# Two neighbouring tokens per partition and 64x64 tiles in the first two batches of a retention and swish kernel

## The chip, the cores and the metric

The kernel runs on one core of a Trainium2 chip, in bf16 matmuls on f32 data from HBM. The metric is device time in microseconds (us) of one execution; smaller is better. Engines: PE (matrix), PEld (its weight loads), DVE (vector), ACT (scalar), POOL (gpsimd) and SP, which issues DMAs.

## The reference

```python
def _attn_ref(q, k, v):                      # q, k, v: 8 batches, 8 heads, 576 tokens, 64
    scores = scale * np.matmul(q, k.transpose(0, 1, 3, 2))
    gamma = 1.0 - 2.0 ** (-5.0 - np.arange(H, dtype=np.float32))
    Dmat = np.where(rel >= 0, gamma[:, None, None] ** rel[None, :, :], 0.0)
    return np.matmul(scores * Dmat, v)
def _moe_ref(x, w_in, w_out, beta):          # x: 4608 x 512; w_in 512 x 2048; w_out 2048 x 512
    h = x @ w_in
    return (h * (1.0 / (1.0 + np.exp(-beta * h)))) @ w_out
```

The first is attention without a softmax, with a decay per head (gamma to the distance, causal). Its heads are laid side by side into x, which goes through two matrices with a swish between them.

## The kernel before

Each batch's first 512 tokens are a block; the last 64 tokens of all eight batches make a ninth block, in four pairs. Attention is done in chunks of 128 tokens. The decay splits into a gain on q (gq) and one on v (gv), so a chunk needs: scores of keys against queries inside the chunk (`a_sc`, tile sc), a causal mask on DVE that also evicts sc from PSUM into R (L332), R times v (`a_O`, tile O), and what earlier chunks add through a 64x64 state per head (`a_cross`). The state is the sum of k times v of the chunks so far (`a_st`, tile st, one PSUM buffer), evicted to sbuf by ACT or DVE after each chunk (L408, L416). O goes to xT (`a_x`), the input of the MLP.

Of q a partition holds four neighbouring tokens (1024-byte runs, `load_q`, L82). Of k and v a partition holds one token of each head, 256-byte runs (`load_kv`, L94). POOL casts k to bf16 (L277) and scales v (L259), DVE scales q in batches 0 and 1 (L251). In these two batches PE turns q and k (`t_q` L301, `t_k` L307) and ACT or DVE evicts (L302, L308); for later batches DMA transposes do it. In batches 0 and 1 a_st multiplies two heads by two heads, 128x128, and keeps the two diagonal blocks; sbd holds them for a_cross with zeros beside them. Later batches use 128x64 tiles for st (L402) and O (L441) and 64x64 tiles for the cross part (L453).

The MLP of a block is `up` (64 matmuls of 512 columns into 16 tiles ph, L473, and a swish on ACT into gT, L475; `up_pair`, L488 and L491, for batch 0's first two tiles) and `down` (64 into 4 tiles po, L506, evicted by L513). Weights come in eight pieces of w_in (L177) and four of w_out (L192), cast by POOL and DVE (L185, L188) or scaled by 1/beta (L200 POOL, L202 ACT, L204 DVE). All loads and most stores go through SP's queue in the order of the code: q, k and v of batch 0, w_in, then w_out, then batch 1 and 2.

The order is written by hand. Batch 0's attention stands as a list of calls, with a few matmuls on a zero tile between them (`warm_up`, L212). After it a list `fill` holds the MLP steps of all blocks; a step is four 512-column matmuls, or four of 256 columns for batch 1's halved up. `merged` walks through fill, and ahead of step n it makes all calls of `streams` that are due (a number at most n). d0 is the index of batch 0's first down step, u1 that of batch 1's first up step (d0 + 16). Each engine takes its own instructions in this order.

```python
    fill += [F(up, 1, fo, 2 * x, 2) for x in range(2) for fo in range(10)]
    fill += [F(up, 1, fo) for fo in range(10, FO)]
```

So batch 1's up takes ten tiles in halves, the first half of the tokens and then the second, and six whole.

Of the kernel before, what the change touches and what calls it, by code (L numbers as in the profile page):

```python
# [19 lines left out]
def kernel(  # L20
# [21 lines left out]
    PC = P // CB  # L42
    TL = S - MB
# [23 lines left out]
    NQ = 6  # L67
    E = CB
# [4 lines left out]
    def load_q(b, us=(0, 1)):  # L73
# [6 lines left out]
        for u in us:  # L80
            w = slice(u * HP, (u + 1) * HP)
            nc.sync.dma_start(t[:, w].rearrange("p h i d -> p h (i d)"),  # L82
                              q[b, w, :MB, :].rearrange("h (p i) d -> p h (i d)", i=CB))

# [12 lines left out]
    ahead = [(0, 0), (0, 1), (1, 0), (1, 1), (2, 0), (3, 0), (2, 1), (3, 1)]  # L97
    keys_first = [(0, 0), (1, 0), (0, 1), (1, 1), (2, 0), (3, 0), (2, 1), (3, 1)]
# [13 lines left out]
    for n, j in ahead:  # L112
        load_kv(n, (j,))
# [7 lines left out]
    pos = consts.tile([P, 2, CB + 1], F32, name="pos")  # L121
    for j, (step, mul) in enumerate(((1, CB), (P, 1))):
        nc.gpsimd.iota(pos[:, j, :CB], pattern=[[step, CB]], base=0, channel_multiplier=mul,
                       allow_small_or_imprecise_dtypes=True)
        for x in range(2):
            nc.gpsimd.iota(pos[x * TL:(x + 1) * TL, j, CB:], pattern=[[0, 1]], base=MB, channel_multiplier=1,
                           allow_small_or_imprecise_dtypes=True)
    lscale = consts.tile([P, 1], F32, name="lscale")
    nc.vector.memset(lscale[:], math.log(scale))
    lg = consts.tile([P, 2, CB + 1, H], F32, name="lg")  # L130
    for h in range(H):
        nc.vector.tensor_scalar(lg[:, :, :, h], pos[:], math.log(1.0 - 2.0 ** (-5.0 - h)), None, ALU.mult)
    gq = consts.tile([P, CB + 1, H], F32, name="gq")
    gv = consts.tile([P, CB + 1, H], F32, name="gv")
    nc.scalar.activation(gq[:], lg[:, 0], ACT.Exp, bias=lscale[:])
    nc.scalar.activation(gv[:], lg[:, 1], ACT.Exp, scale=-1.0)
# [6 lines left out]

    causal = consts.tile([P, P], BF16, name="causal")
    nc.gpsimd.memset(causal[:], 1.0)
    nc.gpsimd.affine_select(out=causal[:], in_=causal[:], pattern=[[1, CB], [CB, PC]], compare_op=ALU.is_ge,
                            fill=0.0, base=0, channel_multiplier=-1)
# [3 lines left out]
    sbds = [consts.tile([P, HP, P], BF16, name=f"sbd{i}") for i in range(NS)]  # L151
# [28 lines left out]
    def cast_w_in(g):  # L180
        t = wts[g]
        f0, fn = pieces[g]
        for ko in range(KO):
# [6 lines left out]
    def load_w_out(g):  # L190
        t = stage.tile([P, KO, d_model], F32, name="wt", tag="wt", bufs=4)
        nc.sync.dma_start(t[:], w_out_r[:, g * KO:(g + 1) * KO, :])  # L192
# [141 lines left out]
    def split(i):  # L334
        return i in (CB - 1, CB + 1)
# [392 lines left out]
```

## Time and profile before

| | |
|---|---|
| runs, median of 3 | 306.67 us (305.7 to 306.93) |
| the profiled execution | 305.54 us |
| its span, first to last instruction | 303.8 us |
| PE, PEld busy | 293.4 us (97%), 151.3 us (50%) |
| DVE, ACT, POOL busy | 108.0, 134.1, 99.9 us |
| granted PE clock | 1.0 in every slice |
| HBM read, written | 36.71 MB, 9.44 MB |

Busy matmuls overlap, so PE's share does not tell how full it is; where PE is the limit is read from the chain that ended last (followed back from the last instruction, at each step to what released it). A group's row gives code line, engine, operation, tiles, count, busy time and the mean of one in ns. A timeline row gives start, length, engine, line, operation, shapes and count; in brackets the idle time ahead of it and what ended it. A windows row gives the stretch, PE, PEld, DVE, ACT and POOL busy (with counts), granted clock, DMA share, GB/s.

### The profile page before, as it was taken

The page shows a single profiled execution, that of the slowest core. Times are in us where ns is not written, and L with a number is a line of the kernel's source. Part 1 is how long each engine was busy: PE and PEld are TensorE (multiplying, and loading weights), DVE is VectorE, ACT ScalarE, POOL GpSimd, SP SyncE. Part 2 cuts the span into 40 slices and gives each one's busy share as a digit, 9 for nine tenths or more (in the row PEclk, how much of TensorE's full clock was granted, in tenths as well). Part 3 has the DMA queues.
Part 4 walks back from the last instruction along what each step waited for, and adds up shares of the span by engine and source line. Part 5 has one row for each costly group of instructions (what it writes and reads, how often), then busy time and mean ns, then how long its engine had stood idle before and what let it go on. Part 6 is the DMA issues. An engine that isn't in the chain of part 4 may idle for free.

```text
span 303.8 us, 5689 instructions
## 1 busy us (share of the span) xinstructions
PE 293.4 (97%) x2311; PEld 151.3 (50%) x2345; DVE 108.0 (36%) x202; ACT 134.1 (44%) x227; POOL 99.9 (33%) x138
## 2 busy tenths in 40 slices
PE   7799999999999999999999999999999999999995
PEld 5544456854544454445444544454455544444444
DVE  6588566504640433133222413151346510020012
ACT  5567546781147313741374127511771058107700
POOL 4666317552840723350308030942342000000000
PEclk9999999999999999999999999999999999999999
DMA  8999999999999999908982889997996110131011
GB/s 210 219 344 363 385 252 244 237 189 243 173 249 265 233 190 230 262 12 158 252 219 66 156 226 243 214 187 184 185 200 112 60 45 0 32 73 35 2 69 69
DMA packets 129210, 53.86 MB, mean 177 GB/s; under 512 B 109968, under 2 KB 122656, under 8 KB 129184
## 3 DMA queue, kind: packets, MB, share of 16 engines
q1 hardware_dynamic: 129152, 53.49, 78.4%
q8 instruction: 18, 0.29, 0.4%
q14 instruction: 8, 0.07, 0.1%
q10 hardware_dynamic: 32, 0.01, 0.0%
HBM read 36.71 MB, written 9.44 MB: 152 GB/s over the span
## 4 chain that ended last, share of the span: by engine, by line
PE 87%; DMA 6%; SPq 4%; issue 1%; POOL 1%; DVE 0%; POOLq 0%
PE po L506 41%; PE ph L473 36%; SPq L94 3%; DMA wt<-in_moe_w_out_dram 3%; PE sc L327 3%; DMA wt<-in_moe_w_in_dram 2%; PE O L441 2%; PE st L402 2%; PE O L453 1%; SPq L177 1%; POOL w_out_sb L200 1%; PE O L376 0%; PE st L405 0%; SPq L82 0%; PE T L307 0%
## 5 line engine op out<-in xcount | busy, mean ns | idle before, releaser
L475 ACT ACTIVATE gT<-ph,beta_sb 128x512 bf16<-128x512 f32 (+1 forms) x152 | 99.5, 659 | 82.2 <-PE ph L473 81.7
L506 PE MATMUL po<-w_out_sb,gT 128*128 128x512 bf16 (+2 forms) x591 | 127.1, 368 | 2.1 <-issue 1.3
L473 PE MATMUL ph<-xT,w_in_sb 128*128 128x512 bf16 (+1 forms) x592 | 125.1, 365 | 0.8 <-issue 0.2
L473 PEld LDWEIGHTS <-w_in_sb 128*128 128x128 bf16 x608 | 58.4, 98 | 63.0 <-DVE w_in_sb L188 0.9
L506 PEld LDWEIGHTS <-gT 128*128 128x128 bf16 x608 | 56.8, 98 | 63.9 <-issue 0.6
L332 DVE TENSOR_TENSOR R<-sc,causal 128x512 bf16<-128x512 f32 x72 | 45.0, 684 | 81.4 <-PE sc L327 80.3
L513 DVE COPY ot<-po 128x512 f32<-128x512 f32 (+2 forms) x34 | 22.4, 657 | 77.2 <-PE po L506 74.4
L277 POOL CAST kn<-kvn 128x512 bf16<-128x512 f32 x32 | 19.5, 612 | 55.5 <-DMA kvn<-in_k_dram 55.1
L259 POOL TENSOR_TENSOR vn<-kvn,gv 128x512 bf16<-128x512 f32 x32 | 33.3, 1042 | 13.1 <-DMA kvn<-in_v_dram 6.3
L251 POOL TENSOR_TENSOR qs<-qn,gq 128x512 bf16<-128x512 f32 x24 | 24.3, 1042 | 35.1 <-DMA qn<-in_q_dram 35.1
L408 ACT CAST sbq<-st 128x256 bf16<-128x256 f32 x18 | 6.6, 369 | 35.8 <-PE st L402 35.8
L461 DVE CAST xT<-O 128x512 bf16<-128x512 f32 x20 | 12.7, 685 | 20.2 <-PE O L453 20.2
L327 PE MATMUL sc<-qT,kT 64*128 64x128 bf16 x256 | 10.8, 218 | 0.7 <-ACT kT L308 0.6
L188 DVE CAST w_in_sb<-wt 64x256 bf16<-64x256 f32 x32 | 10.7, 334 | 1.4 <-DMA wt<-in_moe_w_in_dram 0.3
L461 ACT CAST xT<-O 128x512 bf16<-128x512 f32 x8 | 4.7, 587 | 13.4 <-PE O L453 13.4
L327 PEld LDWEIGHTS <-kT 64*128 64x128 bf16 x288 | 8.2, 94 | 3.8 <-issue 1.7
L185 POOL CAST w_in_sb<-wt 128x256 bf16<-128x256 f32 x16 | 7.2, 469 | 5.3 <-DMA wt<-in_moe_w_in_dram 5.3
L402 PEld LDWEIGHTS <-kn 128*64 128x64 bf16 x192 | 5.1, 110 | 7.6 <-issue 6.4
L212 PE MATMUL ph<-warm 128*128 128x128 f32 (+1 forms) x24 | 6.5, 405 | 1.2 <-DVE warm L119 1.2
L441 PE MATMUL O<-R,vn 128*64 128x128 bf16 x224 | 7.7, 220 | 0.0
L402 PE MATMUL st<-vn,kn 128*64 128x64 bf16 x192 | 7.4, 200 | 0.0
L266 POOL TENSOR_TENSOR kn<-tln,gq 128x512 bf16<-128x512 f32 x4 | 4.2, 1042 | 9.8 <-DMA tln<-in_q_dram 5.9
(69 smaller groups left out, 103.4 us busy)
## 6 DMA issues: line engine op xcount, KB each, us to landing
qn<-in_q_dram SPq DMA_DIRECT2D x16, 512.0 KB, 5.8
kvn<-in_k_dram SPq DMA_DIRECT2D x32, 256.0 KB, 5.1
kvn<-in_v_dram SPq DMA_DIRECT2D x32, 256.0 KB, 5.0
out_dram<-ot SPq DMA_DIRECT2D x31, 256.0 KB, 2.8
wt<-in_moe_w_out_dram SPq DMA_DIRECT2D x4, 1024.0 KB, 9.7
wt<-in_moe_w_in_dram SPq DMA_DIRECT2D x6, 512.0 KB, 8.6
out_dram<-ot SPq DMA_DIRECT2D x9, 128.0 KB, 2.4
wt<-in_moe_w_in_dram SPq DMA_DIRECT2D x4, 256.0 KB, 5.8
```

The costliest lines, as they stand in the source:

```text
L251: e.tensor_tensor(batch[b]["qs"][:, cs, hs], q_tiles[b][:, hs, cs].rearrange("p h i d -> p i h d"), gq[:, cs, hs].unsqueeze(3).to_broadcas ...
L259: nc.gpsimd.tensor_tensor(live[i]["vn"][:], kv_tiles.pop(i)[:, 1], gains(gv, c), ALU.mult)
L277: nc.gpsimd.tensor_copy(kn[:, c % 2], t[:, 0])
L327: nc.tensor.matmul(view(sc[j][:, p, :]), L["kT"][r, p, :], rhs, start=True, stop=True, skip_group_check=True)
L332: nc.vector.tensor_tensor(R[:, j], sc[j][:], m_b, ALU.mult)
L402: nc.tensor.matmul(st[j * D:(j + 1) * D, p, :D], L["kn"][:, 2 * p + j, :], L["vn"][:, 2 * p + j, :], start=(c == 0 and p == 0), stop=True, ...
L441: nc.tensor.matmul(out4(i, p, hh), L["vn"][:, 2 * p + j, :], rhs if b is None else rhs.rearrange("k (i s) -> k i s", i=CB), start=c % 2 == ...
L461: (nc.scalar.copy if n == 1 else nc.vector.tensor_copy)(to, O.rearrange("k p i s -> k p (i s)") if b is None else O[:])
L473: nc.tensor.matmul(ph, w_in_sb[:, ko, fo * P:(fo + 1) * P], xts[m][:, ko, :, w], start=(ko == 0), stop=(ko == KO - 1))
L475: nc.scalar.activation(gts[m][:, fo, :, w], ph, ACT.Silu, scale=beta_sb[:, fo:fo + 1])
L506: nc.tensor.matmul(po[:, :nn], gT[:, fo, ms, :], w_out_sb[:, fo, n0:n0 + nn], start=(fo == 0), stop=(fo == FO - 1))
L513: (nc.scalar.copy if m == 0 else nc.vector.tensor_copy)(ot, po[:, :nn])
```

## The change

Batches 0 and 1 work in two spans of 256 tokens. A partition of k and v holds two neighbouring tokens (`load_span`), for q of batch 1 too. A span's partitions 0 to 63 are its first chunk and 64 to 127 its second, so scores (`sc_span`) and R times v (`O_span`) are done with 64 keys at a time on 64x64 tiles, twice as many as before. The state is summed anew for each of a span's two chunks (`st_span`, 128x64 or 64x64 tiles), which makes 96 matmuls of 64 columns a batch in place of 16 of 128. In batch 0 keys carry the gain, values are cast only, and both are worked on by halves of the heads; q's scaling is shared by DVE and POOL. Keys of batch 1 are cast by ACT and POOL. Batch 1's up takes 14 tiles in halves, and the steps of its spans have other due times. w_out is loaded in eight parts, batch 2's transposes and preparation come later in the order. The small operations on beta go to DVE. V, A and Z stand for DVE, ACT and POOL.

```diff
         for u in us:
+            if b == 1:
+                nc.sync.dma_start(t[:, :, 2 * u:2 * u + 2].rearrange("p h i d -> p h (i d)"),
+                                  q[b, :, u * W:(u + 1) * W, :].rearrange("h (p i) d -> p h (i d)", i=2))
+                continue
...
+    def load_span(b, j, cc, hs):
+
+        if (b, j, cc) not in spans:
+            spans[b, j, cc] = stage.tile([P, H, 2, D], F32, name="kvn", tag="kvn", bufs=NQ)
+        nc.sync.dma_start(spans[b, j, cc][:, hs].rearrange("p h i d -> p h (i d)"),
+                          (k, v)[j][b, hs, cc * W:(cc + 1) * W, :].rearrange("h (p i) d -> p h (i d)", i=2))
...
+    for j, g in ((0, 0), (0, 1), (1, 0), (1, 1)):
+        for cc in range(2):
+            load_span(0, j, cc, both[g])
...
     def load_w_out(g):
         t = stage.tile([P, KO, d_model], F32, name="wt", tag="wt", bufs=4)
-        nc.sync.dma_start(t[:], w_out_r[:, g * KO:(g + 1) * KO, :])
+        for w in range(0, KO, 2):
+            nc.sync.dma_start(t[:, w:w + 2], w_out_r[:, g * KO + w:g * KO + w + 2, :])
...
+        nc.vector.tensor_tensor(tiny[:], beta_sb[:], beta_sb[:], ALU.mult)
+        nc.vector.tensor_scalar(tiny[:], tiny[:], 1e-24, 1e-12, ALU.is_lt, ALU.mult)
+        nc.vector.tensor_tensor(beta_sb[:], beta_sb[:], tiny[:], ALU.add)
...
-        if b < 2:
-            hs, cs = slice(n // 2 * HP, (n // 2 + 1) * HP), slice(n % 2 * 2, n % 2 * 2 + 2)
-            e = nc.vector
+        if b == 0:
+            hs, cs, e = slice(n // 2 * HP, (n // 2 + 1) * HP), slice(n % 2 * 2, n % 2 * 2 + 2), (nc.vector, nc.gpsimd)[n % 2]
+        elif b == 1:
+            hs, cs, e = slice(n % 2 * HP, (n % 2 + 1) * HP), slice(n // 2 * 2, n // 2 * 2 + 2), nc.vector
         else:
             hs, cs, e = slice(0, H), slice(n, n + 1), nc.gpsimd
+        gain = gq2 if b == 1 else gq
...
+    def pre_span(b, j, cc, hs, e, gain=False):
+
+        if (b, cc) not in pair:
+            pair[b, cc] = [sb.tile([P, 2, H, D], BF16, name="kn", tag="kn", bufs=4),
+                           sb.tile([P, 2, HP, P], BF16, name="kT", tag="kT", bufs=4),
+                           sb.tile([P, 2, H, D], BF16, name="vn", tag="vn", bufs=3)]
+        put(e, pair[b, cc][2 * j][:, :, hs], spans[b, j, cc][:, hs].rearrange("p h i d -> p i h d"),
+            gv2[:, 2 * cc:2 * cc + 2, hs].unsqueeze(3).to_broadcast([P, 2, hs.stop - hs.start, D]) if gain else None)
...
+    def t_q(b, u, tag, e):
+
+        T = psum.tile([P, CB, 2, P] if b == 0 else [P, 2, HP, P], BF16, name="T", tag=tag, bufs=BANKS[tag])
+        for i in range(T.shape[1]):
+            for p in range(T.shape[2]):
+                nc.tensor.transpose(T[:, i, p, :], heads(batch[b]["qs"][:, i if b == 0 else 2 * u + i], p + (2 * u if b == 0 else 0)), ident[:])
+        qT = batch[b]["qT"]
+        evict(e, qT[:, :, 2 * u:2 * u + 2] if b == 0 else qT[:, 2 * u:2 * u + 2], T[:])
+
+    def t_k(b, cc, ps, tag, e):
+
+        kn, kT = pair[b, cc][:2]
+        T = psum.tile([P, 2, len(ps), P], BF16, name="T", tag=tag, bufs=BANKS[tag])
+        for i in range(2):
+            for n, p in enumerate(ps):
+                nc.tensor.transpose(T[:, i, n, :], heads(kn[:, i], p), ident[:])
+        evict(e, kT[:, :, ps[0]:ps[-1] + 1, :], T[:])
+
+    def q_span(b, c, r, p):
+
+        qT = batch[b]["qT"]
+        return qT[r, :, p, c * PC:(c + 1) * PC] if b == 0 else qT[r, c // 2 * 2:c // 2 * 2 + 2, p, c % 2 * D:(c % 2 + 1) * D]
+
+    def by(b, o):
+        return o.rearrange("k (i s) -> k i s", i=CB if b == 0 else 2)
+
+    Rs, Os, begun = {}, {}, set()
+
+    def sc_span(b, cc, g, tag, via=()):
+
+        kT = pair[b, cc][1]
+        Rs[b, cc, g] = R = sb.tile([P, 2, 2, 2, P], BF16, name="R", tag="R", bufs=4)
+        sc = [psum.tile([P, 2, 2, P], F32, name="sc", tag=tag, bufs=BANKS[tag]) for _ in range(2)]
+        for n, i in ((n, i) for n in range(2) for i in range(2)):
+            p = 2 * g + n
+            for j, h in ((0, 0), (1, 1), (0, 1), (1, 0)):
+                r = slice(j * D, (j + 1) * D)
+                nc.tensor.matmul(by(b, sc[j][h * D:(h + 1) * D, n, i, :]), kT[r, i, p, h * D:(h + 1) * D], q_span(b, 2 * cc + h, r, p),
+                                 start=True, stop=True, skip_group_check=True)
+        for j in range(2):
+            nc.vector.tensor_tensor(R[:, j], sc[j][:], cuts[b][:].unsqueeze(1).to_broadcast([P, 2, 2, P]), ALU.mult)
...
+    def O_span(b, cc, g):
+
+        vn, R = pair[b, cc][2], Rs[b, cc, g]
+        for n, i in ((n, i) for n in range(2) for i in range(2)):
+            p = 2 * g + n
+            for j, h in ((0, 0), (1, 1), (0, 1), (1, 0)):
+                r, hh = slice(h * D, (h + 1) * D), j ^ p % 2
+                key, o = region(b, 2 * cc + h, p)
+                nc.tensor.matmul(o[hh * D:(hh + 1) * D], vn[r, i, 2 * p + j, :], by(b, R[r, j, n, i, :]),
+                                 start=begins(key, (hh,)), stop=False, skip_group_check=True)
+
+    def cross_span(b, c, ps):
+
+        cc, h = (c - 1) // 2, (c - 1) % 2
+        for p in ps:
+            s = sbds[cc][:, h, p // 2, p % 2 * 2:p % 2 * 2 + 2, :]
+            key, o = region(b, c, p)
+            nc.tensor.matmul(o, s.rearrange("k h d -> k (h d)"), q_span(b, c, slice(0, P), p),
+                             start=begins(key, (0, 1)), stop=True, skip_group_check=True)
+
+    def st_span(b, cc, ps, es, end=True):
+
+        n = len(ps)
+        st = psum.tile([P, 2, n, D], F32, name="st", tag="st", bufs=1)
+        for x in range(2):
+            terms = [(d, i, slice(0, P)) for d in range(cc) for i in range(2)] + \
+                    [(cc, i, slice(0, P if x else D)) for i in range(2)]
+            for m, p in enumerate(ps):
+                for t, (d, i, r) in enumerate(terms):
+                    kn, _, vn = pair[b, d]
+                    for j in range(2):
+                        nc.tensor.matmul(st[j * D:(j + 1) * D, x, m, :], kn[r, i, 2 * p + j, :], vn[r, i, 2 * p + j, :],
+                                         start=(x == 0 and m == 0 and t == 0), stop=True, skip_group_check=True)
+        ns = 2 - cc
+        for j, y in ((0, slice(0, 4, 3)), (1, slice(1, 3))):
+            r = slice(j * D, (j + 1) * D)
+            if n == 2:
+                evict(es[j], sbds[cc][r, :, ps[0] // 2, y], st[r, :ns])
+            else:
+                evict(es[j], sbds[cc][r].rearrange("k x g y d -> k (x g) y d")[:, :, y], st[r, :ns].rearrange("k x (u y) d -> k (x u) y d", y=2))
+        if cc:
+            evict(es[2], ends[b][:, ps[0]:ps[-1] + 1], st[:, 1])
+
+    def x_span(b, key, es):
+
+        for h, e in enumerate(es):
+            O = Os[b, key][h]
+            if b == 0:
+                evict(e, xt(b)[:, 2 * key:2 * key + 2].rearrange("k p i (c h s) -> k (p i) c h s", c=2, h=2)[:, :, :, h],
+                      O.rearrange("k p i c s -> k (p i) c s"))
+            else:
+                evict(e, xt(b)[:, :, 2 * key:2 * key + 2, h * D:(h + 1) * D], O[:])
...
     def up(m, fo, c0=0, cn=CB):
         if m not in gts:
             gts[m] = sb.tile([P, FO, CB, P], BF16, name="gT", tag="gT", bufs=2)
-        w = slice(c0 * PC, (c0 + cn) * PC)
-        ph = psum.tile([P, CB, P], F32, name="ph", tag="mm", bufs=3)
-        ph = ph.rearrange("f i s -> f (i s)")[:, :cn * P].rearrange("f (i s) -> f i s", i=CB)
+        w = slice(c0, c0 + cn)
+        ph = psum.tile([P, CB, P], F32, name="ph", tag="mm", bufs=3)[:, :cn]
         for ko in range(KO):
-            nc.tensor.matmul(ph, w_in_sb[:, ko, fo * P:(fo + 1) * P], xts[m][:, ko, :, w],
+            nc.tensor.matmul(ph, w_in_sb[:, ko, fo * P:(fo + 1) * P], xts[m][:, ko, w],
                              start=(ko == 0), stop=(ko == KO - 1))
-        nc.scalar.activation(gts[m][:, fo, :, w], ph, ACT.Silu, scale=beta_sb[:, fo:fo + 1])
+        nc.scalar.activation(gts[m][:, fo, w], ph, ACT.Silu, scale=beta_sb[:, fo:fo + 1])
 
     phs = {}
...
+    V, A, Z = nc.vector, nc.scalar, nc.gpsimd
+
     warm_up(5)
     betas()
+    pre_q(0, 0)
+    pre_q(0, 1)
     betas_safe()
-    for n in range(4):
-        pre_q(0, n)
-    t_q(0, 0)
+    t_q(0, 0, "mm", A)
+    pre_q(0, 2)
+    pre_q(0, 3)
+    warm_up(2, 128)
+    pre_span(0, 0, 0, both[0], V, True)
+    t_q(0, 1, "mm", A)
+    t_k(0, 0, (0, 1), "mm", V)
+    pre_span(0, 0, 1, both[0], Z, True)
+    pre_span(0, 0, 0, both[1], Z, True)
+    pre_span(0, 0, 1, both[1], Z, True)
+    sc_span(0, 0, 0, "sc")
+    t_k(0, 1, (0, 1), "mm", A)
     warm_up(1, 128)
-    t_q(0, 1)
-    pre(0)
-    t_k(0)
-    warm_up(2, 128)
-    a_sc(0)
-    a_st(0)
-    pre(1)
-    t_k(1)
+    sc_span(0, 1, 0, "O")
+    pre_span(0, 1, 0, both[0], Z)
+    pre_span(0, 1, 1, both[0], Z)
+    t_k(0, 0, (2, 3), "mm", A)
     warm_up(1, 128)
-    a_cross(0, True)
-    a_O(0)
-    a_x(0)
-    a_sc(1)
-    a_cross(1, True)
-    pre(2, (0,))
-    t_k(2)
-    a_st(1)
-    a_O(1)
-    pre(3, (0,))
-    a_sc(2)
-    t_k(3)
-    a_x(1)
+    sc_span(0, 0, 1, "sc")
+    t_k(0, 1, (2, 3), "mm", A)
     warm_up(1, 128)
-    a_sc(3)
-    a_cross(2, True)
-    pre(2, (1,))
-    a_st(2)
-    a_O(2)
-    a_x(2)
-    pre(3, (1,))
-    warm_up(2, 128)
-    a_cross(3, True)
-    a_O(3)
-    a_x(3)
-    cast_w_in(0)
-    a_st(3)
+    st_span(0, 0, (0, 1), (A, A))
+    new_span_O(0, 0, ("O", "O"))
+    O_span(0, 0, 0)
+    sc_span(0, 1, 1, "mm")
+    pre_span(0, 1, 0, both[1], Z)
+    pre_span(0, 1, 1, both[1], Z)
+    st_span(0, 1, (0, 1), (A, A, A))
+    O_span(0, 1, 0)
+    cross_span(0, 2, (0, 1))
+    cross_span(0, 1, (0, 1))
+    st_span(0, 0, (2, 3), (A, A))
+    cross_span(0, 3, (0, 1))
+    x_span(0, 0, (A, V))
+    cast_w_in(0, (0, 1))
+    new_span_O(0, 1, ("sc", "sc"))
+    O_span(0, 0, 1)
+    st_span(0, 1, (2, 3), (A, A, A))
+    O_span(0, 1, 1)
+    cross_span(0, 1, (2, 3))
+    cross_span(0, 2, (2, 3))
+    up_pair(0, 0, 0)
+    cross_span(0, 3, (2, 3))
+    x_span(0, 1, (V, A))
+    cast_w_in(0, (2, 3))
...
+    cut_of(1)
...
-    fill = [F(up_pair, 0, fo, u) for fo in (0,) for u in range(2)] + [F(up, 0, fo) for fo in range(2, FO)]
+    fill = [F(up_pair, 0, 0, 1)] + [F(up, 0, fo) for fo in range(2, FO)]
...
     u1 = len(fill)
-    fill += [F(up, 1, fo, 2 * x, 2) for x in range(2) for fo in range(10)]
-    fill += [F(up, 1, fo) for fo in range(10, FO)]
+    NH = 14
+    fill += [F(up, 1, fo, 2 * x, 2) for x in range(2) for fo in range(NH)]
+    fill += [F(up, 1, fo) for fo in range(NH, FO)]
     fill += [F(down, 1, ms, f0) for ms in range(MB // P) for f0 in range(0, FO, 4)]
-    base = {1: u1 + 10}
+    base = {1: u1 + NH}
...
+    def span_sc(cc):
+        sc_span(1, cc, 0, "sc")
+        sc_span(1, cc, 1, "O")
+
+    def span_out(cc):
+
+        new_span_O(1, cc, ("sc", "sc"))
+        O_span(1, cc, 0)
+        O_span(1, cc, 1)
+        if cc:
+            cross_span(1, 2, range(HP))
+
+    def span_rest(cc):
+
+        cross_span(1, 2 * cc + 1, range(HP))
+        x_span(1, cc, (A, V))
+
+    def kv1(cc):
+        return [(10.3, F(load_q, 1, (cc,)))] + [(10.3, F(load_span, 1, j, cc, all_h)) for j in range(2)]
+
+    def span_steps(cc, q0, k0, v0, s0, t0, o0, x0):
+
+        return [(q0, F(pre_q, 1, 2 * cc)), (q0, F(pre_q, 1, 2 * cc + 1)), (q0 + .5, F(t_q, 1, cc, "O", V)),
+                (k0, F(pre_span, 1, 0, cc, both[0], A)), (k0, F(pre_span, 1, 0, cc, both[1], Z)),
+                (k0 + .5, F(t_k, 1, cc, range(HP), "O", A)),
+                (v0, F(pre_span, 1, 1, cc, both[0], V, True)), (v0, F(pre_span, 1, 1, cc, both[1], Z, True)),
+                (s0, F(span_sc, cc)), (t0, F(st_span, 1, cc, range(HP), (A, A, A))), (o0, F(span_out, cc)),
+                (x0, F(span_rest, cc))]
 
     streams = [[(0, F(load_w_out, 0)), (0.1, F(cast_w_in, 2)), (2.1, F(cast_w_in, 3)), (2.2, F(load_w_out, 1)),
                 (4.1, F(cast_w_in, 4)), (6.1, F(cast_w_in, 5)), (6.2, F(load_w_out, 2)), (8.1, F(cast_w_in, 6)),
                 (10.1, F(cast_w_in, 7)), (10.2, F(load_w_out, 3))],
                [(d0 - 4 + 3.3 * g, F(cast_w_out, g)) for g in range(WG)],
-               [(10.3, F(load_q, 1))] + [(10.3, F(load_kv, CB + n, (j,))) for n, j in keys_first],
+               kv1(0), kv1(1),
                [(10.4, F(load_q, 2))] + [(10.4, F(load_kv, 2 * CB + n)) for n in range(2)],
-               [(d0 + 8.6, F(load_kv, 2 * CB + 2)), (d0 + 12.6, F(x_q, XB, 0)), (d0 + 12.7, F(x_q, XB, 1)),
-                (d0 + 13.6, F(x_k, XB, 0)), (d0 + 13.8, F(load_kv, 2 * CB + 3)),
+               [(d0 + 8.6, F(load_kv, 2 * CB + 2)), (u1 + 6.1, F(x_q, XB, 0)), (u1 + 6.2, F(x_q, XB, 1)),
+                (u1 + 6.3, F(x_k, XB, 0)), (u1 + 6.5, F(load_kv, 2 * CB + 3)),
                 (base[2] - 4.5, F(release, 4)), (base[2] + 8, F(release, 4))],
-               [(d0 + 7, F(pre_q, 1, n)) for n in range(4)] + [(d0 + 12.5, F(pre_q, XB, n)) for n in range(4)] + [(d0 + 11.6, F(t_q, 1, 0)), (d0 + 12.6, F(t_q, 1, 1))],
-               [(d0 + 8, F(pre, 4, (0,))), (d0 + 8, F(pre, 5, (0,))), (d0 + 9, F(pre, 4, (1,))), (d0 + 9, F(pre, 5, (1,))),
-                (d0 + 12.7, F(t_k, 4)), (d0 + 14, F(t_k, 5)), (d0 + 14, F(a_sc, 4)), (d0 + 15, F(a_sc, 5)),
-                (d0 + 15, F(a_st, 4)), (d0 + 15.9, F(second, 4))],
-               [(d0 + 10, F(pre, 6, (0,))), (d0 + 10, F(pre, 7, (0,))), (d0 + 12, F(pre, 6, (1,))), (d0 + 12, F(pre, 7, (1,))),
-                (d0 + 15.95, F(t_k, 6)), (u1 + 1, F(t_k, 7)), (u1 + 2, F(a_sc, 6)), (u1 + 3, F(a_sc, 7)),
-                (u1 + 4, F(a_st, 6)), (u1 + 7, F(second, 6))]]
+               [(u1 + 6, F(pre_q, XB, n)) for n in range(4)],
+               span_steps(0, d0 + 12.5, d0 + 14.3, d0 + 15.4, d0 + 15.7, d0 + 15.8, d0 + 15.85, d0 + 15.9),
+               span_steps(1, u1 + 2, u1 + 3, u1 + 5, u1 + 6, u1 + 8, u1 + NH - 1, u1 + NH - .1)]
```

## The prediction

> **What bounds the kernel now.** I read three views in this order: the chain that ended last, PE's timeline of the first 35 us, and the DMA rate by stretch. The page's share of 97% for PE is only an average; the chain says where PE is the limit:
>
> ```profile
> 11.98 1.14 SPq L177
> ...
> 14.70 7.06 DMA wt<-in_moe_w_in_dram
> ...
> 22.18 9.78 DMA wt<-in_moe_w_out_dram
> ...
> 32.10 2.52 POOL w_out_sb L200 x2
> 34.66 7.50 PE po L506 x34
> ```
>
> (columns: start, length, what). The reader is to see that loads stand on the chain up to 32 us and that after 34.66 it is PE until DVE's last copy at 300.88. From there a microsecond of PE work or PE waiting is a microsecond of time.
>
> ```profile
> 17.89 0.40 PE L405 MATMUL st<-vn,kn 128*128 128x128 bf16 x4
> 18.46 0.59 PE L488 MATMUL ph<-xT,w_in_sb 128*128 128x512 bf16 x2 [0.17 <-ACT xT L386]
> 19.22 1.41 PE L488 MATMUL ph<-xT,w_in_sb 128*128 128x512 bf16 x5 [0.17 <-issue]
> 20.47 12.66 PE L473 MATMUL ph<-xT,w_in_sb 128*128 128x512 bf16 x55
> 32.96 1.55 PE L506 MATMUL po<-w_out_sb,gT 128*128 128x512 bf16 x6
> 34.66 9.22 PE L506 MATMUL po<-w_out_sb,gT 128*128 128x512 bf16 x41 [0.15 <-POOL w_out_sb L200]
> ```
>
> Batch 0's attention ends near 18.4, then PE is dense. Neighbouring 512-column matmuls start 0.216 us apart in the trace, and eight of the 64 of batch 0's up are done at 20.47 (one record is missing), so PE stands as if dense from 20.47 - 8 x 0.216 = **18.74**. The kernel can gain ahead of that point, and lose behind it.
>
> ```profile
> 6.00:14.00 8.00, 5.85 (x76) 4.06 (x76) 4.61 (x8) 4.11 (x8) 5.30 (x9) 1.00 1.38 218
> 18.00:26.00 8.00, 7.63 (x35) 2.93 (x36) 7.06 (x22) 5.68 (x10) 4.76 (x12) 1.00 1.09 348
> 30.00:36.00 6.00, 5.79 (x27) 2.50 (x27) 3.60 (x7) 3.87 (x6) 2.74 (x3) 1.00 1.04 387
> ```
>
> The last number is GB/s; the DMA share before it is full in all three. k and v move in 256-byte runs in the first stretch, w_in in 1024 in the second, w_out in 2048 in the third.
>
> **Loads.** Each of 16 engines needs 256 x 16 / 218 = 18.8 ns for a 256-byte packet, 47.1 for 1024 and 84.7 for 2048: a line, 9.4 ns + 0.0368 a byte. So a 512-byte packet is estimated at 28.2 ns, 290 GB/s. Batch 0's k and v (2.10 MB) then take 7.2 us in place of 9.6: all that follows lands 2.4 us earlier. Ends: 0 (rate stays 218) and 3.6 (348). The Trainium skill, "DMA: Bandwidth & Descriptors", Specifications, puts line rate at 512 bytes and more; by that it would be the end of 3.6, and no run here shows loads of this size yet.
>
> **Start, batch 0.** In before POOL's waits show k and v landing every 1.2 us from 7.47. Now 256 KB pieces land each 0.91: keys 7.1, 8.0, 8.9, 9.8, values 10.8 to 13.5, first w_in quarter 14.3. But three helpers stand between. POOL scales three key halves (1.042 each, row L259): 8.0 to 11.1; four plain value casts (0.61, L277) end at 14.1. ACT's fourth kT eviction (0.58, L308) ends about 12.6. From there the states are a chain, since psum st has one buffer: evict 0.37 + 0.37 (L416) to 13.3; 32 st matmuls 0.55 to 13.85; three evictions (0.27 each, estimated between the rows of 0.585 at 512 columns and 0.366 at 256) to 14.65; st to 15.0; two evictions to 15.75, then xT on ACT (0.59) to 16.35; st to 16.4, O and cross to 16.95. Four up matmuls (0.86) to 17.85, cross, the last xT on DVE (0.69, L461) to 18.7, and behind it on DVE the two w_in casts of ko 3 (0.35 each: eight took 2.81) to 19.4. Then PE is dense with five matmuls done: 19.4 - 5 x 0.216 = 18.3, 0.4 earlier. With 1.5 us earlier w_in, whose casts held PE 0.4 in before (waits of L473 and L488 on DVE), and earlier halves of w_out (0.15 to 0.2 of wait at 34.66 goes), I take **-0.8**. Ends: -3.75, if nothing but the first cast weights (14.9) held it, and +0.8, if each of eight hand-overs in the state chain costs 0.2 more than I allowed. I am nearer the second end since each link has its row.
>
> **Batch 1, first span: where it loses.** The order of the changed PE stream is: 52 po, 8 T, 8 po, 8 T, 4 po, then 32 sc, 32 st, 32 O, 4 cross, and only then the first up of batch 1, which needs their xT. In before 4 po stand between each of these. Here nothing covers DVE. sc starts at S; the first 16 end S+0.42 (four 64x64 tiles start together each 56 ns, as below). Four masks on DVE, 0.65 apart (2.59 for four at 47.32), end S+3.0; the last O and cross to S+3.5; xT 0.69 and hand-over: up at S+4.35. PE's own work in it is sc 0.45, st 0.51, O 0.45, cross 0.22 = 1.63; the other 2.7 is idle or drain. Ahead of S, ACT's kT of 1024 columns (1.01, L302) has 0.86 of po as cover: with the hand-over 0.25 of wait. From the 48th po to the first up before takes 43.73 to 51.11 = 7.38 us. After: 16 po 3.45 + 16 T 0.90 + 0.25 + 4.35 = 8.95: **+1.55**. Ends +0.6 (R's first half is enough for half of O, and DVE, ACT overlap better) and +2.2.
>
> **Batch 1, rest of its up.** Before: 51.11 to 68.01 = 16.9. After: up itself is the same 13.8 (112 matmuls of 256 columns at 0.108, 8 of 512); T 0.9; sc 0.55, st 64 x 16 ns + 0.12 = 1.15, O 0.55, cross 0.5: 17.45. The last cross and xT now stand directly ahead of the first up that reads them (ACT: a gT of 0.47, then xT 0.59): 0.9 of wait; kT 0.25; and ACT, whose 13 half gT took 5.56 (0.43 each, PE's half is 0.43), gets key casts and state evictions among 28 halves, not 20: 0.3. Sum 18.9: **+2.0**. Ends +0.5 (no wait, ACT keeps up) and +3.
>
> **64x64 tiles.** The trace has the form: L453, four tiles starting 3 ns apart and fours each 56 ns, 14 ns a matmul; before's pairs (L441) also come each 56, so 64 small sc or O matmuls cost what 32 did. st costs 96 x 16 = 1.54 in place of 16 x 56 ns = 0.9, counted above. The Trainium skill, "TensorE: Matmul & The Clock Gate", section "Wait — 56ns, not 53.3ns?", gives about 25 ns as the least distance of starts. The trace disagrees for neighbours in different tiles (3 ns). By the rule, batch 1 would cost 2 us more. It is a rival below.
>
> Other edits: betas_safe goes from POOL to DVE, three 16-column operations ahead of 6.2 us where DVE waits for q; the second q half is what it waits for. w_out in eight issues rather than four stays behind the same cast waits on SP. x_q and pre_q of batch 2 come later in SP's and POOL's order (about 5 us), behind them key casts, but the first scores of batch 2 are at 69.3 and POOL was through at 65.2 with a wait for q that now ends earlier: nothing, up to +1 if the transposes are late. Batches 2 to 7 keep their work.
>
> **Sum.** -0.8 + 1.55 + 2.0 = **+2.75 us** on the profiled execution of 305.54 (span 303.8): 308.3. That execution lies 1.1 below the median of the three runs; on the median of 306.67 it is **309.4**, which I give.
>
> **Rivals.**
> - *The start wins it back* (chance 0.20). The mechanism is the state chain of batch 0: if its links hide and PE is dense from 15.0, the start gives -3.75, and with +3.55 behind it the time is 306.5, not slower. For it: values land by 13.5 at the latest. Against: one st buffer, DVE's casts behind the last xT. It decides from a dense PE earlier than 15.2. With the low end of the second span it is 305.0. Runs at 348 GB/s belong here: worth 1.2 at most, and POOL and ACT stand behind them, so 0.7: 308.7 by itself.
> - *The waits of batch 1 are half of mine* (0.15): 309.4 - 1.7 = 307.7. For it: ACT and DVE split xT. Against: the four masks on one engine.
> - *Small tiles don't overlap in fours* (0.10): 224 matmuls at 28 ns (a pair's half) in place of 15: +2.9, some 0.7 of it inside the mask wait: 311.6. For it: different banks and lengths. Against: L453.
> - *The loads don't get faster* (0.05): w_in and w_out as before, start +0.5: 310.7.
> - The forecast: 0.50.
>
> A measurement of this kernel tells 0.5% (1.5 us) from no change. Forecast, small tiles and slow loads are slower (0.65); the half waits and 0.08 of the first rival are the same (0.23); the other 0.12 of it, with the second span at its low end too, is faster (0.12). The range leaves out the lowest of the first rival and the worst ends of both spans: **304.8 to 312.0**.
>
> **What would show it.** Loads: 290 GB/s in the stretch from 6 to 12 us, and the last value cast ending near 14.1. Start: dense PE at about 19.4. First span: some 2.5 us of PE idle ahead of batch 1's first up, released by DVE's R and xT. Second: a wait of 0.9 on xT half way in the 256-column matmuls. Small tiles: four starts per 56 ns. Wrong I would be if PE is dense before 17, or if other work fills PE while DVE masks.

## The result, and the profile after

The changed kernel takes 326.74 us (median of four, 324.68 to 329.55) against 306.75 for the kernel before beside it: a ratio of 1.064 (95% interval 1.058 to 1.070). The 329.55 is a slow run, at clock 0.967, and the ratio is taken without it. The kernel is slower, as forecast, but by 20 us and not by 2.75, far outside the range. The profiled execution took 326.36, its span is 324.5 (before 303.8), its mean granted clock 0.978 (before 1.000).

Five marks on PE divide the span; the dense start is taken as in the prediction, eight matmuls of 0.216 back from where eight are done. All columns but the last are read from the timelines; 256-byte runs is the best of the experiments below.

| stretch, us | before | after | difference | forecast | 256-byte runs |
|---|---|---|---|---|---|
| to the dense start of batch 0's up | 18.74 | 23.60 | +4.86 | -0.4 | 20.78 |
| to its first po | 14.22 | 13.82 | -0.40 | -0.4 | 14.05 |
| to batch 1's first up | 18.15 | 19.71 | +1.56 | +1.55 | 17.87 |
| to batch 1's first po | 16.90 | 22.29 | +5.39 | +2.0 | 18.89 |
| to the end | 235.79 | 245.08 | +9.29 | 0 | 237.51 |
| span | 303.8 | 324.5 | +20.7 | +2.75 | 309.1 |

The chain that ended last, of after (start, length, what):

```profile
6.34 0.23 DVE tiny L254
6.59 0.98 DVE tiny L255
7.59 0.18 DVE beta_sb L256
...
25.50 12.09 PE ph L555 x56
...
53.06 2.50 DVE R L389 x4
55.60 0.41 PE O L417 x15
56.38 0.69 DVE xT L347
57.07 2.84 DVE qs L283 x2
...
237.71 1.02 POOL vn L316
238.75 0.62 SPq L123
...
242.86 1.30 SPq L334
244.27 3.27 DMA kT<-kn
247.58 0.61 PE sc L479 x8
```

No load of w_in or w_out is on it any more. Near its start stand the three small operations on beta (6.34 to 7.77), which the prediction had put where DVE waits anyway; DVE's second half of q comes behind them. The masks R and xT ahead of batch 1's first up are there as forecast; behind them stand two scalings of q on DVE; and at 237.71 there is a chain that the prediction did not have: a tail's value on POOL, six load issues, a transpose, its DMA. Its head, in the timeline of after, and then the row of before for the same 16 scores, which wait for nothing:

```profile
237.68 1.04 POOL L316 TENSOR_TENSOR vn<-tln,gv 128x512 bf16<-128x512 f32 x1 [11.76 <-PE O L524]
...
246.45 0.61 PE L479 MATMUL sc<-kT 64*128 64x128 bf16 x8 [5.96 <-DMA kT<-kn]
247.58 0.61 PE L479 MATMUL sc<-kT 64*128 64x128 bf16 x8 [0.52 <-DMA kT<-kn]
248.13 6.36 PE L588 MATMUL po<-w_out_sb,gT 128*128 128x512 bf16 x20
```

```profile
229.01 0.66 PE L327 MATMUL sc<-kT 64*128 64x128 bf16 x16
```

POOL waits 11.76 us until PE's outputs free a vn buffer; behind it on POOL stand the next tails, and the loads that refill their tiles; PE runs dry for 5.96 us. In after each tail takes a whole tile of the shape [P, 2, H, D] out of three; before, the tails took single ones out of six.

The start in after: ACT's fourth eviction of kT, PE's timeline, and then stretches of 3.41 us (busy time of PE, PEld, DVE, ACT, POOL with counts, then the granted clock, DMA share, GB/s):

```profile
13.56 0.59 ACT L347 COPY kT<-T 128x512 bf16<-128x512 bf16 x1 [0.83 <-PE T L364]
...
17.90 0.25 PE L417 MATMUL O<-R,vn 64*64 64x128 bf16 x3
19.30 0.38 PE L417 MATMUL O<-R,vn 64*64 64x128 bf16 x13 [1.16 <-issue]
19.61 1.56 PE L440 MATMUL st<-vn,kn 128*64 128x64 bf16 x32
...
24.47 1.02 PE L570 MATMUL ph<-xT,w_in_sb 128*128 128x512 bf16 x4 [0.67 <-ACT xT L347]
25.33 1.03 PE L555 MATMUL ph<-xT,w_in_sb 128*128 128x512 bf16 x4
```

```profile
13.01:16.42 3.41, 3.14 (x116) 2.59 (x106) 2.68 (x5) 1.41 (x4) 2.30 (x5) 1.00 1.10 347
16.42:19.83 3.41, 2.02 (x60) 1.30 (x50) 1.40 (x3) 2.02 (x6) 2.68 (x10) 1.00 1.10 349
...
53.97:57.38 3.41, 1.67 (x39) 1.06 (x38) 2.58 (x5) 1.66 (x3) 2.52 (x3) 1.00 1.07 203
241.70:245.11 3.41, 0.00 (x0) 0.00 (x0) 0.00 (x0) 0.00 (x0) 1.65 (x2) 1.00 1.08 198
```

PE's scores start at 9.94, 11.36 and 12.78: each round of transposes, eviction and scores takes 1.42 us. Later, after three matmuls of an output tile, PE stops for 1.16 us and waits for nothing that the profile shows ("issue"). And the granted clock, 1.00 throughout in before, is 0.50 in three stretches, which begin exactly where the last three of these windows end: 19.83 to 23.24, 57.38 to 60.79 and 245.11 to 251.94. Each is once or twice 3.41 us long. The Trainium skill, "TensorE: Matmul & The Clock Gate", Part 1, gives the window as 3413 ns, running freely; the length agrees with the trace. It has the clock fall after an idle window. Here PE was busy for 2.02 and 1.67 us of two of them.

### The profile page after: what moved, and what is told of

Same layout as the page of the kernel before. It is cut to its first block, busy times and chain, and to the rows that moved or that the text cites. A ratio compares the mean times of both kernels' runs of the same rounds, so it can differ in the third digit from the quotient of the medians.

```text
span 324.5 us, 6323 instructions
## 1 busy us (share of the span) xinstructions
PE 305.4 (94%) x2645; PEld 159.2 (49%) x2645; DVE 111.4 (34%) x202; ACT 136.0 (42%) x233; POOL 99.1 (31%) x139
## 4 chain that ended last, share of the span: by engine, by line
PE 90%; DVE 3%; ACT 2%; SPq 2%; issue 1%; DMA 1%; POOL 0%; POOLq 0%; ACTq 0%; DVEq 0%
PE po L588 39%; PE ph L555 37%; PE sc L479 2%; PE O L524 2%; PE st L440 2%; PE st L497 2%; PE ph L244 2%; SPq L123 1%; DVE qs L283 1%; DMA kT<-kn 1%; ACT kT L347 1%; PE O L536 1%; DVE R L389 1%; PE ph L570 1%; PE sc L386 1%
## 5 line engine op out<-in xcount | busy, mean ns | idle before, releaser
L588 PE MATMUL po<-w_out_sb,gT 128*128 128x512 bf16 (+2 forms) x608 | 130.7, 372 | 0.0
L555 PE MATMUL ph<-xT,w_in_sb 128*128 128x512 bf16 (+1 forms) x624 | 127.7, 363 | 1.8 <-ACT xT L347 0.8
L555 PEld LDWEIGHTS <-w_in_sb 128*128 128x128 bf16 x624 | 60.5, 99 | 63.3 <-DVE xT L347 1.9
L484 DVE TENSOR_TENSOR R<-sc,causal 128x512 bf16<-128x512 f32 x56 | 34.8, 684 | 80.9 <-PE sc L479 71.3
L283 POOL TENSOR_TENSOR qs<-qn,gq 128x512 bf16<-128x512 f32 x26 | 27.2, 1078 | 36.9 <-DMA qn<-in_q_dram 36.9
L326 POOL CAST kn<-kvn 128x512 bf16<-128x512 f32 x24 | 15.0, 628 | 49.3 <-DMA kvn<-in_k_dram 49.2
L307 POOL TENSOR_TENSOR vn<-kvn,gv 128x512 bf16<-128x512 f32 x24 | 25.4, 1060 | 14.6 <-issue 7.6
L389 DVE TENSOR_TENSOR R<-sc,cut 128x512 bf16<-128x512 f32 x16 | 10.1, 685 | 4.3 <-PE sc L386 4.1
L316 POOL TENSOR_TENSOR vn<-tln,gv 128x512 bf16<-128x512 f32 x4 | 4.2, 1042 | 21.7 <-PE O L524 21.7
L244 PE MATMUL ph<-warm 128*128 128x256 f32 (+1 forms) x20 | 6.6, 473 | 1.2 <-DVE warm L135 1.2
```

Of the source, the lines that this page charges most:

```text
L283: e.tensor_tensor(batch[b]["qs"][:, cs, hs], q_tiles[b][:, hs, cs].rearrange("p h i d -> p i h d"), gain[:, cs, hs].unsqueeze(3).to_broadc ...
L307: nc.gpsimd.tensor_tensor(live[i]["vn"], kv_tiles.pop(i)[:, 1], gains(gv, c), ALU.mult)
L326: nc.gpsimd.tensor_copy(kn[:, c % 2], t[:, 0])
L484: nc.vector.tensor_tensor(R[:, j], sc[j][:], m_b, ALU.mult)
L555: nc.tensor.matmul(ph, w_in_sb[:, ko, fo * P:(fo + 1) * P], xts[m][:, ko, w], start=(ko == 0), stop=(ko == KO - 1))
L588: nc.tensor.matmul(po[:, :nn], gT[:, fo, ms, :], w_out_sb[:, fo, n0:n0 + nn], start=(fo == 0), stop=(fo == FO - 1))
```

## The experiments

My theory after the result had four parts: buffers of the tails, st matmuls that switch between 128 and 64 rows, waits without cover in batch 1, and the clock that falls behind waits. The rival for all was that the tiles of 64x64 are slow in themselves. It falls by after's own trace: fours start 56 ns apart, as forecast.

**e1, two tails share one pair buffer.**

```
-            vn = sb.tile([P, 2, H, D], BF16, name="vn", tag="vn", bufs=3)[:, 0]
+            if c % 2 == 0:
+                pair[b, c // 2] = sb.tile([P, 2, H, D], BF16, name="vn", tag="vn", bufs=3)
+            vn = pair[b, c // 2][:, c % 2]
```

> The changed kernel, but two tails share one pair buffer of values (before, each tail took a whole pair buffer, so three tails filled the pool). Theory, buffers: POOL's wait of 11.8 us for PE's O of the tails goes, and with it 9 us of PE idle from 238 to 247.6 and the slow clock behind it; about 316 to 317 us. Rival, order of SP: the last transposes are late since batch 2's steps stand later in the queue, buffers or not; then about 326 us as the changed kernel.

Measured 319.55, ratio 1.045 (1.039 to 1.051). From batch 2's first st to the last matmul it takes 232.73 us (after 240.63, before 231.65): 7.9 of the 9 us at the tails are this one buffer, with the halved clock behind its wait. The whole is only 7.2 shorter; in this execution the two earlier halved stretches are 6.83 us each. The timeline of e1:

```profile
239.50 1.04 POOL L318 TENSOR_TENSOR vn<-tln,gv 128x512 bf16<-128x512 f32 x1 [4.08 <-PE O L526]
...
242.67 0.40 PE L481 MATMUL sc<-kT 64*128 64x128 bf16 x8 [0.36 <-DMA kT<-kn]
243.59 0.40 PE L481 MATMUL sc<-kT 64*128 64x128 bf16 x8 [0.52 <-DMA kT<-kn]
```

**e2, the first span earlier in the stream, with po between its steps.** `span_steps(0, d0 + 9.5, d0 + 9.9, d0 + 11, d0 + 12, d0 + 13, d0 + 14.9, d0 + 15)`

> The changed kernel with the steps of batch 1's first span 3 to 4 down steps earlier, so that down matmuls stand between scores, states, O and the first up. Theory, no cover: the 2.3 us of PE waits at 53.8 to 57.1 go, and with them the 3.4 us of half clock at 57.4 (1.7 us): 322 to 323 us. Rival, late data: k and v of batch 1 land too late for it and PE waits for DMA or POOL instead: 326 us or more.

Measured 326.56, 1.068 (1.065 to 1.070): no gain in all. In its place the edit works: from batch 0's first po to batch 1's first up 17.63 us against 19.71, no wait for DVE there (0.24 for kT and 0.16 without a releaser are left), and no halved clock at 57. But in this execution the clock was halved from 12.85 to 26.51, far ahead of the edit, and the first po came 2.2 later.

**e3, states by rows.** The loop over terms stands outside, the loop over head pairs inside, so that matmuls of 64 rows stand together.

> The changed kernel with the state's matmuls ordered so that all with 128 rows of keys come first and then those with 64, in place of switching between them for each pair of heads. Theory, row switches: the 64 state matmuls of batch 1's second span take 1.1 to 1.2 us in place of 2.1, the 32 in batch 0 0.6 to 0.7 in place of 1.16; about 1.5 to 2 us in all, 324.5 us. Rival, size: the matmuls are slow by themselves (33 ns each) and nothing changes: 326 us.

Measured 324.89, 1.062 (1.058 to 1.066). The 64 st matmuls of batch 1, e3 and then after:

```profile
62.76 1.44 PE L440 MATMUL st<-vn,kn 128*64 128x64 bf16 x64
```

```profile
64.39 2.13 PE L440 MATMUL st<-vn,kn 128*64 128x64 bf16 x64
```

The same matmuls in another order save 0.69, and 32 of batch 0 take 0.93 instead of 1.16. The Trainium skill, "TensorEngine Tiling (Array Packing)", Key Properties, says that a change of tiling mode drains TensorE, without a price; here a switch costs about 0.12 us (four matmuls in 0.18 where 0.064 would do).

**e4, all three, and the second span moved too** (its q scaled during batch 0's down, its outputs two fills earlier).

> The three edits together, and the second span's O, cross and xT two half tiles earlier, its q scaled ahead of POOL's work on batch 2. If the causes add: 9.3 + 4 + 1.7 + 1.5 below 326.5, so about 310 us. Rival, one cause behind the other: PE waits in another place for what the first wait had covered, and 313 to 316 us remain.

Measured 312.97, 1.022 (1.017 to 1.027): 13.8 of 20 us are back, not the forecast 16.5. Batch 1 from its first up to its first po takes 18.90, with 0.4 us of wait left in it (0.23 for kT, 0.19 for ACT's cast of k).

**e5 to e8** start from e4 and look at the start. e5 puts six more calls of warm_up(1, 128) into PE's waits; e6 also moves betas_safe behind the first xT; e7 puts 16 unused matmuls of 2 columns ahead of the second q transposes; e8 loads batch 0's k and v by one DMA for each neighbouring token:

```
...
+        for i in range(2) if b == 0 else ():
+            nc.sync.dma_start(spans[b, j, cc][:, hs, i], src[:, :, i])
...
```

> Base is the version with the tails paired, the first span covered, the states by rows and the second span moved (312.97 us, its own start-up at half clock from 9.62 to 16.45 us, first st at 16.40, dense start with eight of its matmuls done at 25.78). Six calls of warm_up(1, 128) are put into PE's waits of the start: three ahead of the second q transposes, two ahead of the first k transposes, one ahead of the first scores. Clock theory: the granted clock stays 1.00 until past 17 us, the 5.35 us that PE is busy between 11.04 and 16.40 shrink to about 3.2, the first st comes at 14.0 to 14.5 (the last value cast ends at 14.04), and the time falls by 2.1 to 310.9 (309.9 to 311.9). Rival, the start hangs on its chain of evictions and casts and not on the clock: clock 1.00, first st still past 16, time 312.5 to 313.5. Second rival, waits are not what lowers the clock: it is 0.50 again within 9 to 17 us, 312.5 to 313.5.

> As the run before it with the warm-ups, and the three small DVE operations that make beta safe stand after the first output eviction of batch 0 instead of ahead of DVE's second half of q. DVE's q half then ends about 1.3 us earlier (7.1 instead of 8.4) and the second q transposes start at about 7.1 instead of 8.46. Theory, DVE's first k half waits for its load (it started at 8.32, POOL's at 8.11 when k landed): the first scores come only 0.2 to 0.3 earlier, time 0.2 below the run before it. Rival, the delayed q is what the start hangs on: the first scores come 1.2 earlier and the time is 1.2 below.

> Same base (312.97), with 16 more bf16 matmuls of 2 columns (32 PE instructions with their weight loads) ahead of the second q transposes, which do nothing for the result. There PE waits anyway. Fetch theory: PE stops where its instructions run out, so the wait without a releaser (0.78 us after the third matmul of O(0,0,1) in the base) stands 16 matmuls earlier, after the fifth matmul of the second st of the first half (key pairs 2 and 3); time within 0.5 us of 312.97. Rival, the wait belongs to that output tile (its bank, its operands): it stays after the third matmul of O(0,0,1).

> Same base (312.97), with k and v of batch 0 loaded by one DMA for each of the two neighbouring tokens, so in runs of 256 bytes into the same places; nothing else changes. Load theory of my forecast: these 2.1 MB go at 218 GB/s instead of 290, the last value cast ends 2 to 2.4 us later than 14.04, and as the first st stands at 16.40 for other reasons, the dense start comes at most 0.9 later: 313.9 (313.0 to 314.4). Rival A, the start follows the loads one to one: 315.2. Rival B, the runs are worth nothing here: within 0.4 of 312.97.

e5: 312.61 (1.017 to 1.026). In its profile the clock is 1.00 through the start, the first st at 14.04 and the dense start 2.2 earlier than in e4, as forecast; but the median did not move: the clock of the other three runs is 0.986 to 0.993. e6: 312.10 (1.017 to 1.027). DVE's second half of q ended at 7.06, as forecast, but the first scores came only 0.13 earlier than in e5. That does not clear q, since the added warm-ups held PE until the second q transposes began at 8.26. In e12, with betas_safe moved alike and no such warm-ups, the first scores start at 9.50, against 9.94 in after: the place of betas_safe is worth some 0.4 us there. It was not tried alone.

e7: 311.34 (1.012 to 1.022), from two runs. The stop went where the fetch theory put it:

```profile
16.87 0.28 PE L447 MATMUL st<-vn,kn 64*64 64x64 bf16 x5 [0.23 <-ACT end L354]
17.95 0.62 PE L447 MATMUL st<-vn,kn 64*64 64x64 bf16 x11 [0.81 <-issue]
```

After the fifth st, 16 matmuls ahead of its old place: PE stops at a place in its instructions, not at a tile. Other runs agree: with 12 matmuls more ahead of it (e5, e10) the stop stands after the ninth st, with 10 more (e9, e11) after the eleventh. One 16 KB packet on the instruction queue ran from 15.28 to 16.36 in e7, 16.74 to 17.83 in after, and PE goes on 1.4 to 1.6 us behind its end in after, e1, e4, e5, e7 and e9. That PE waits for this packet is inferred from the times; no run moved the packet alone.

e8: 310.79 (1.011 to 1.017), not slower than e4. The stretches of e8 and then of e4, and e8's last value cast:

```profile
8.00:12.00 4.00, 2.64 (x55) 1.94 (x55) 2.86 (x6) 1.65 (x3) 2.70 (x3) 1.00 1.35 218
```

```profile
8.00:12.00 4.00, 2.19 (x32) 1.59 (x33) 2.48 (x4) 1.01 (x1) 3.89 (x4) 0.70 1.22 290
```

```profile
16.01 0.61 POOL L295 CAST vn<-kvn 128x512 bf16<-128x512 f32 x1 [0.48 <-DMA kvn<-in_v_dram]
```

The loads are at 218 GB/s again and the last cast ends at 16.62 instead of 14.04, and yet the dense start, with the clock at 1.00 and no stop, is the earliest of all (20.78). Its fair neighbour is e6, also at clock 1.00, with 21.19; e4 began at half clock. The longer runs do speed the loads, and at the end they are worth nothing that shows here.

Over the 18 runs of e4 to e8 the time goes with the clock: four at 1.000 took 309.86 to 311.72 (mean 310.7), four at 0.989 took 312.39 to 314.38 (mean 313.5), whatever the kernel.

**e9 to e12** start from e6. e9 issues k's transposes a step ahead of the scores; e10 scales q and k of both last tails ahead of their values; e11 does both; e12 takes out all warm-ups but the first five.

> Base is the version with the extra warm-ups and the late betas (312.10 us median; its profiled run 311.01 at clock 0.999). In the first batch each group of k transposes is issued one step ahead of the scores that use the group before, and two of the three warm-ups between them stay. Theory: PE waited 0.40 us three times for ACT's copy of kT between transposes and scores; that wait goes, the first st falls from 13.91 to 12.3 to 13.0 (the first v half is cast at about 12.3), the dense start (eight done) from 22.92 to 21.7, the time by 1.2 at the same clock: a profiled run of about 309.8 if its clock is 1.00. Rival, POOL's casts of k and v, the last at 14.04, set the pace: the first st moves, but the states of the second span wait for it, and the dense start gains 0.3 at most.

> Same base (312.10; profiled 311.01). Of the two last tails q and k are scaled and cast for both before either's value, which must wait for the pair buffer that batch 7's outputs free (POOL waited 4.07 us on them ahead of the last tail's q and k), and the last transpose goes out 1.5 steps earlier. Theory: the scores' wait for DMA kT (two of 0.5, 1.0 us in all) goes: time 1.0 lower, a profiled run near 310.0. Rival: the values are then what comes last and the wait moves from the scores to the outputs O: within 0.3 of the base.

> The two edits above together. If each theory holds they add, since one is in the first 25 us and the other past 225: 2.2 below the base, median 309.9, 308.8 in runs whose clock is 1.00. That is still 0.9 to 1.2% above the kernel before: what stays is the first batch's small matmuls (about 0.8), batch 1's uncovered stages (1.5) and the tails' later place (0.7).

> Same base (312.10; its four runs had clocks 0.999, 1.000, 0.994, 0.989), with every warm-up of the start but the first five taken out, so that PE idles where they stood; nothing that the result needs changes. Clock theory: PE's idle share in the first 15 us is what brings the granted clock to 0.50, so most runs fall to 0.97 to 0.99, with a half-clock stretch between 7 and 24 us in the profiled one, and the median is 314 to 316. Rival, the clock falls by chance whatever PE does there: the same spread of clocks as the base, 311.0 to 312.5.

e9: 312.75 (1.020 to 1.025), nothing gained, where 1.2 us were forecast. The first st came at 12.83 (e6 13.91), and then:

```profile
16.14 0.49 PE L442 MATMUL st<-vn,kn 64*64 64x64 bf16 x11 [0.23 <-ACT end L349]
17.89 0.32 PE L442 MATMUL st<-vn,kn 128*64 128x64 bf16 x5 [1.25 <-issue]
```

PE reached its stop sooner and stood longer, and behind the stop the clock was halved from 17.87 to 24.70; its four runs have 0.984 to 0.992. e10: 312.34 (1.015 to 1.022); the scores' wait fell from 1.0 to 0.5 and not to nothing, too little to be seen in the time. e11: 311.89 (1.017 to 1.022), not the forecast 309.9. e12: 313.63 (1.023 to 1.027), all four runs at 0.973 to 0.978, where e6 has 0.989 to 1.000; the stretches of e12:

```profile
5.99:9.40 3.41, 2.03 (x21) 1.13 (x21) 2.24 (x3) 2.12 (x3) 3.08 (x4) 1.00 1.22 291
9.40:26.47 17.07, 14.73 (x254) 9.87 (x256) 10.60 (x25) 6.13 (x17) 11.98 (x29) 0.50 1.01 301
```

Without them the clock falls in every run, and for 17 us in the profiled one: idleness brings it down, not chance alone.

**e13 and e14** are the changed kernel with 24 unused matmuls of 512 columns ahead of the scores of the last pair of tails (e13) and of the first (e14).

> The changed kernel itself (326.74 us), with 24 matmuls of 512 columns whose product is not used put on PE ahead of the scores of the last two tails, where PE stood idle for 5.96 us waiting for kT; the wait, its buffers and all other work stay. Theory: part of what that wait costs is the granted clock, which was 0.50 for 6.83 us right behind it. With PE busy (24 x 0.216 = 5.2 us) the clock stays 1.00 there; the eight scores take 0.40 instead of 0.61 twice and the 20 down matmuls 4.49 instead of 6.36, so 2.3 us come back: 324.4. The scores still start at about 246.4. Rival, the halved clock hangs on what runs behind the wait or on the loads beside it: it is 0.50 past 245 all the same, 326.7. Second rival, the fillers end later than the transposes: PE starts the scores after 246.5 and the gain is eaten.

> The changed kernel (326.74 us) with the 24 unused matmuls now ahead of the scores of the first pair of tails: the 5.96 us wait stands there, not ahead of the last pair, where the run before had put them and where they only lengthened PE's work by 5.3 us. Same theories: clock from idleness, the clock stays 1.00 past 245 us, scores at 246.4 as before, 2.3 us come back: 324.4, or 330.0 less 2.3 against the run before. Rival, the halved clock has another cause: 0.50 again past 245 and 326.7.

e13: 332.20 (1.081 to 1.089). I had taken the wrong pair: the matmuls ran in 5.34 us where PE was dense, and the time rose by 5.5. e14: 326.35 (1.065 to 1.069). Its timeline:

```profile
242.31 5.34 PE L759 MATMUL ph<-w_in_sb,ident 128*128 128x512 bf16 x24
248.56 0.40 PE L479 MATMUL sc<-kT 64*128 64x128 bf16 x8 [0.90 <-DMA kT<-kn]
249.74 0.40 PE L479 MATMUL sc<-kT 64*128 64x128 bf16 x8 [0.78 <-DMA kT<-kn]
250.07 4.49 PE L588 MATMUL po<-w_out_sb,gT 128*128 128x512 bf16 x20
```

The clock stays at 1.00 and the 20 down matmuls take 4.49 instead of 6.36, though the scores still wait for the same DMA. From the four po ahead of the fillers to the tails' first O it takes 13.04 (241.45 to 254.49) against 14.94 in after: 1.9 of the forecast 2.3. So the clock's price is separate from the wait's. The total did not fall to the forecast 324.4: in this profile the two earlier halved stretches are 6.83 us each instead of 3.41.

## Why the prediction was right and wrong

The spans differ by 18 us more than forecast: 9.3 of them lie at the tails, 5.3 in the start and 3.4 in the rest of batch 1.

- **First span of batch 1: right in mechanism, and in size partly by luck.** R three times (0.96 in all) and xT (0.79) are the releasers, and e2 gave it back. The row's +1.56 against +1.55 hides two misses. From the 48th po, 47.79 in after by 48 po of 0.216, to the first up it takes 9.34 us, where I had 8.95: +1.96 on before. The 48 po themselves take 0.40 less than in before, of which I had put 0.15 to 0.2 into the start's -0.8. Of the 2.5 us of idle PE that I expected to see, 1.75 are waits.
- **Loads: right, and beside the point.** 291 GB/s from 8 to 12 us where I had estimated 290, last value cast by 14.5 where I had 14.1. e8 shows that this moves nothing.
- **Start: the failed step is "From there the states are a chain".** It began late: ACT's fourth kT eviction ended at 14.15 and not at 12.6, since the three rounds ahead of it went one behind the other, 1.42 us each; in e9, with the transposes ahead, the first st came 0.9 earlier than in after, and the stop took that back. And I priced evictions and let PE's own matmuls lie in them. From the first st at 13.73 to the first up at 22.08 PE waited 1.66 us, 1.16 of it in the stop; the rest it was busy with 96 st (3.84 us), 80 O and scores (2.5) and ten cross. Between 14 and 21 us e6 has 189 PE matmuls where before has 68. With full clock, st by rows and no stop, e8 is still 2.0 later than before; the other 2.8 of after are the stop (1.16), the halved clock and the row switches, none of which was a term of the sum. The operations on beta, which I put at nothing, stand on the chain.
- **Rest of batch 1: right kind, wrong size,** +5.39 for +2.0. The xT wait (0.82 for 0.9) and kT (0.23 for 0.25) are there. Missed: st at 33 ns for 16 (2.13 for 1.15), the halved clock at 57.38, and T's wait for DVE's q. In e3, whose clock stayed at 1.00 there, this wait is 1.1, and the whole stretch takes 21.07: 1.2 less, of which the st are 0.69, so the clock and the wait partly cover each other. DVE's two scalings of q took 2.92 in after, beside POOL's for batch 2 (54.86 to 59.35); in e4, moved away from them, they take 0.69 each. e4 is still 2.0 above before, 1.6 without its waits, where I had 0.55; that part was not split.
- **"Batches 2 to 7 keep their work": true, and the step that failed most.** They keep their work, but the tails lost their buffers, 9.29 us. The code showed it: the tag of vn went from six single tiles (L261 of before) to three pairs, and a tail takes one with half of it unused. I followed the pair buffers only through batches 0 and 1.
- **The clock had no term.** I priced every wait at its length. Where waits leave part of a window empty, the 3.41 or 6.83 us behind it can run at half clock.
- **Small tiles**: fours each 56 ns, as the row of before had it; that rival is false. So is the first: the start did not win anything back. The loads did get faster, and batch 1 did not cost half of what I had put.

No version beats the kernel before: the fastest, e8, is 1.4% slower (1.1 to 1.7%). What keeps it there in its profile is the start (2.0), batch 1 (1.7) and 1.6 behind the last matmul. The tails are back: from batch 2's first st to the last matmul it takes 231.76, against 231.65 in before, and the scores there wait for no DMA. Behind the last matmul the span goes on for 4.6 us, against 3.0 in before and 3.3 to 3.8 in the other profiles; whether that belongs to e8 or to this execution is open.

What stays open: how much work in a window keeps the clock up. In the profiles it fell behind windows with PE busy for 0 to 2.56 us of 3.41, and stayed up in the first 14 us of before, with 2.35 to 2.62 in such stretches; whether busy time or the part of the array in use counts was not tried. Nor was the start's cost split by kind of matmul at full clock.

## What to carry to other kernels

When a tile grows, list every user of its tag to the last line of the program, and count its buffers in units of what each user takes, since the cost comes where the fewest buffers are left, not where the edit is. Faster loads did not help here, where PE had its own matmuls to do: count PE's instructions in the stage, not just the hand-overs. And a wait on PE in a stage of small matmuls can have a second price behind it, in windows of 3.41 us at half clock.

## What was not expected of the hardware

- PE can stop at a fixed place in its program, for 0.56 to 1.29 us, and goes on 1.4 to 1.6 us behind a 16 KB packet of the instruction queue; that its instructions ran out is the likeliest reading. In e2 and e8, where PE got there 1.8 and 1.7 us behind the packet's end, no stop shows.
- Halved clock for one to five windows (3.41 to 17.07 us), in most profiles though PE was over half busy in the window before, and with PE busy for 5.92 of the 6.83 us inside (e9). The same program had a clock of 0.989 in one execution and 0.998 in the next (e4).
- A switch between 128 and 64 rows costs about 0.12 us.
- DVE's scaling of q went from 0.69 to 1.4 us beside POOL's, and POOL's from 1.04 to 1.49 beside DVE's (1.52 at the start).
